# Moving the mixture stage's gathers, scatters and decode writes between queues and out of run-time branches

## The chip, the cores and the metric

The kernel runs on one core of a Trainium2 chip. The metric is device time in microseconds of one execution; the kernel before was executed three times, and its median is 681.64 us. One further execution was taken with the hardware profiler, and all rows below come from that one. A core has five instruction streams: PE (TensorE, matrix products and transposes), ACT (ScalarE), DVE (VectorE), POOL (GpSimd) and SP (SyncE, which here only starts transfers). Transfers are started from a queue of SP, of ACT or of POOL and run on 16 DMA engines that all queues share. Each stream works through its instructions in order and stands at the first one whose inputs are not there.

## What is computed

The reference is attention over a local window with a few global keys, then a mixture of eight experts, then a Fourier mixing step with a two-layer network. The change touches the mixture alone:

```python
logits = np.einsum('bsd,de->bse', x, w_gate)          # B=2, S=768, D=512, E=8
...
        p = softmax(logits[b, s])                      # e is the arg max, or the previous token's expert
        h = np.maximum(x[b, s] @ w1[e], 0.0)           # D -> F=1024
        out[b, s] = p[e] * (h @ w2[e])                 # F -> D
```

Which tokens go to which expert is known only at run time. For the network at the end, `w_ch1` and `w_ch2` arrive as 64-bit words that have to be decoded to 32-bit numbers.

## The kernel before, in words

Attention writes each token's row (512 numbers and the 8 probabilities) to a scratch tensor `xs` in device memory, and for every expert a list of its tokens. The mixture then runs expert by expert, `Moe.expert(e, n, more)` for e = 0 to 7 (called here e0 to e7), where `n` is the number of 128-token chunks that expert e has, as a register. In the profiled execution e1, e2, e3 and e5 have more than one chunk, e4 and e6 have one.

**Tokens.** `gathers(e)` (L1157) issues three indirect DMAs on POOL's queue (L1134), one per possible chunk, which bring the rows of expert e from `xs` into the tiles `xg`. Chunks 0 and 1 of every expert use the same two tiles; chunk 2 alternates between two. `tokens(e)` (L1171) transposes chunks 0 and 1 of `xg` on PE (L1165, four transposes each), splits the result into a high part on ACT (`xh`, L1168) and a low part on DVE (`xl`, L1169), copies the probabilities to `pc` on DVE (L1181) and, at its end, issues `gathers(e + 1)`. `tokens(e + 1)` runs as background work inside expert e, so `gathers(e + 2)` is issued inside expert e.

**Three branched parts.** For e1 to e6 an expert consists of three parts that are run-time branches (`tc.If`), each with an arm that is left out:

1. L1360 to L1363: with n > 1 `wide()`, the first product for 256 tokens (`first256`, L1224); else `narrow(y)`, which does both products for 128 tokens, and the next expert's `tokens` with them.
2. `third()` (L1292): the product `weight(e, (2,))`, a copy of `pc` by DVE, and with n > 2 a third chunk.
3. L1366 to L1369: with n > 1 `seconds(y, z)`, the second product of chunk 0 into the PSUM tile `y` and of chunk 1 into `z` (`second`, L1204), with `tokens(e + 1)` in the background; else one idle product into `z` (`keep_busy`, L50).

Behind the third part ACT scales `y` and `z` by `pc` into SBUF (`write`, L1187), and POOL scatters both to the result `x2` by indirect DMA (L1192).

**Weights.** `Ring` streams the weights through four staging buffers `raws` of 1 MB (`load`, on SP's queue, L987 for expert weights and L991 for the 64-bit words) in a fixed order. `take` splits an expert's 1 MB piece into two casts on ACT (L1049) and two subtractions on DVE (L1051), and then loads the piece four places on into the freed buffer. Expert e splits the weights of expert e + 1: those of the first product in part 1 (`first`), those of the second in part 3 (`then`). Eight pieces of 64-bit words are decoded in between (`d` units: ACT L1082, then DVE L1091, L1093, L1095 and L1097). A decoded piece, the tile `dec` of 512 KB with two buffers, is written to a scratch tensor `wmf` by a DMA on POOL's queue (L1015), behind the load that takes the freed staging buffer. Expert parts 1 of e1, e2, e3 and e5 end with such a piece, and parts 3 of e2 and e3 do.

The order in which instructions of background work stand between the products is the program's own: after every third product of the second stage, and twice per pair of 128-column blocks in the first, the background advances by fixed steps. In part 3 the order on ACT is: first cast of the piece, `xh` of chunk 0, second cast, `xh` of chunk 1, the other two casts, and the decode's first step.

Of the kernel before, what the change touches and what calls it, by code (L numbers as in the profile page):

```python
# [11 lines left out]
F32 = mybir.dt.float32  # L12
# [5 lines left out]
AF = mybir.ActivationFunctionType  # L18
# [27 lines left out]
def keep_busy(nc, st, ps, n):  # L46

    x = st.busy
    for _ in range(n):
        nc.tensor.matmul(ps, x[:, :1].to_broadcast([P, P]), x.unsqueeze(1).to_broadcast([P, 8, D]), start=True, stop=True)  # L50
# [887 lines left out]
class Ring:  # L938
# [63 lines left out]
    def take(self, kind, n, cols=1024, follow=True, eng=None, first=None, part=(0, 1), free=lambda: True):  # L1002

        nc = self.tc.nc
        r = self.at[kind, n]
        raw = self.st.raw[r % PIECES]
        if kind == "d":
            words, t = self.start(r)
            yield
            for k, _ in enumerate(self.bits(words, t)):  # L1010
                if k != 0:
                    yield
            self.load(r + PIECES)

            nc.gpsimd.dma_start(self.st.wm[n // 2, :, n % 2 * (PW // 2):(n % 2 + 1) * (PW // 2)], t)  # L1015
            return
        hi, lo = self.get(kind, n)
        w = TW if kind == "t" else PW
        if kind == "m" and MIX[n][0] >= EARLY:
            w = PW // 2  # L1020
            held = []

            def place():
                for k, t in held:
                    cs = slice(k * w, k * w + w)
                    nc.scalar.copy(hi[:, cs], t)
                    self.behind.append((lo[:, cs], t, hi[:, cs].bitcast(F32), n if k else None))
                held.clear()

            for k in range(2):  # L1030
                words, t = self.start(r + k)
                held.append((k, t))
                for j, cost in enumerate(self.bits(words, t)):
                    if j == 0:
                        self.small()
                    yield cost
                self.load(r + k + PIECES)
                yield 0
                if len(held) < 2:
                    self.start(r + k + 1)  # L1040
                if free():
                    place()
            while not free():
                yield 0
            place()
            return
        for c in range(int(part[0] * w), int(part[1] * w), cols):
            cs = slice(c, min(c + cols, w))
            (first or nc.scalar.copy)(hi[:, cs], raw[:, cs])  # L1049
            yield  # L1050
            (eng() if callable(eng) else eng or nc.vector).tensor_tensor(lo[:, cs], raw[:, cs], hi[:, cs].bitcast(F32), op=ALU.subtract)  # L1051
            yield
        if follow:
            self.load(r + PIECES)
# [46 lines left out]
class Moe:  # L1101
# [69 lines left out]
    def tokens(self, e):  # L1171
        for c in range(2):
            yield from self.turn(e % 2, c, self.place(e, c + (e == 0)))
            yield
        self.weight(e, range(2) if e else (1, 2))
        if e + 1 < E:
            self.gathers(e + 1)

    def weight(self, e, cs):
        for c in cs:  # L1180
# [81 lines left out]
    def expert(self, e, n, more):  # L1262
        tc, ring = self.tc, self.st.ring
        nc = tc.nc
        pc, ent = self.pc[e % 2], self.ent[e % 4]
        w1, w2 = rows(self.st, 4 * e), rows(self.st, 4 * e + 2)
        bg = Background()

        def chain(*gs):
            for g in gs:  # L1270
                yield from g


        at = 0 if e else 1
        step = lambda: bg.step(2)
        spare = self.ps_more, "more"

        def result(c, h, y, ys, *more):
            if isinstance(y, tuple):
                y = y[0].tile([P, DM], F32, name=y[1])  # L1280
            self.second(*h, w2, y, *more)
            bg.drain()
            if not ys:
                return
            last = e == LAST and c == 1
            write = lambda: self.write(y, pc[:, c:c + 1], ent[:, c, 1:2], ys, "first" if last else None)
            if last:
                self.finish = write
            else:
                write()  # L1290

        def third():  # L1292
            self.weight(e, (2,))

            with tc.If(n > 2):  # L1295
                if e < LAST:
                    for _ in self.turn(2, 0, self.place(e, 2)):
                        pass
                late = self.first128(w1, *self.more, spare, spare)
                result(2, self.more[1], spare, "more", lambda: None, late)  # L1300
                if e == LAST:
                    self.rest(more)

        own = lambda s, c: [t[:, :, c * P:(c + 1) * P] for t in s]
        hs = self.hh[0], self.hl[0]
        first, then = ([ring.take(*u, follow=e < LAST) for u in units] for units in ring.plan[e])

        def wide():
            bg.add(chain(*first))
            calls = iter(range(8))  # L1310
            n = 2 + (len(first) > 3)
            self.first256(e, lambda: bg.step(n) if e or next(calls) > 1 else None)
            bg.drain()

        def anew(units):
            for u in units:
                if u[0] == "d":
                    ring.begun.pop(ring.at[u], None)

        def narrow(y):  # L1320
            units = [u for part in ring.plan[e] for u in part]
            anew(units)
            takes = {u: ring.take(*u) for u in units}
            d = [takes[u] for u in units if u[0] == "d"]
            bg.add(chain(*(takes["e", 4 * e + 4 + k] for k in range(2))))
            h = own(hs, 0)
            late = self.first128(w1, own((self.xh[e % 2], self.xl[e % 2]), 0), h, (self.ps_h, "h"), (self.ps_x, "xtp"), bg.step,
                                 [self.place(e, 2)[:, :DM], self.work.tile([P, DM], F32, name="ys", bufs=2)])
            bg.drain()
            then = chain(*(takes["e", 4 * e + 6 + k] for k in range(2)), *d)  # L1330
            bg.add(then)
            calls = iter(range(8))

            def behind():
                if next(calls) == TOKENS:
                    bg.add(self.tokens(e + 1))
                bg.step()

            result(0, h, y, None, behind, late)

        def seconds(y, z):
            anew(ring.plan[e][1])
            bg.add(self.tokens(e + 1))
            bg.add(chain(*then))
            result(at, own(hs, 0), y, "" if e else "ys", step)
            if e:
                result(1, own(hs, 1), z, None)

        if e == 0:
            self.entries(2)  # L1350
            wide()
            seconds((self.ps_y, "y"), None)
            with tc.If(n > at + 1):
                result(at + 1, own(hs, 1), spare, "more")
            return
        if e < LAST:
            if e + 2 < E:
                self.entries(e + 2)
            y = self.ps_y.tile([P, DM], F32, name="y")
            with tc.If(n > 1) as arm:  # L1360
                wide()
            with arm.Else():
                narrow(y)  # L1363
            third()
            z = self.ps_more.tile([P, DM], F32, name="more")
            with tc.If(n > 1) as arm:  # L1366
                seconds(y, z)
            with arm.Else():
                keep_busy(nc, self.st, z, 1)  # L1369
            for c, t, k in ((0, y, "ys"), (1, z, "more")):  # L1370
                self.write(t, pc[:, c:c + 1], ent[:, c, 1:2], k)
            return

        bg.add(self.turn(2, 0, self.place(e, 2)))
        for c in range(2):
            x, h = (own(s, c) for s in ((self.xh[e % 2], self.xl[e % 2]), (self.hh[0], self.hl[0])))
            late = self.first128(w1, x, h, (self.ps_h, "h"), (self.ps_x, "xtp"), step, [x[:, :DM] for x in self.xg[:2]])
            if c == 0:
                third()
                bg.add(chain(*first))  # L1380
            result(c, h, (self.ps_y, "y"), "ys", step, late)
            if c == 0:
                self.fetch(0)
# [56 lines left out]
    def run(self):  # L1440
# [15 lines left out]
        keep_busy(nc, st, spare, WARM[1])  # L1456
        for _ in self.tokens(0):
            pass
        keep_busy(nc, st, spare, WARM[2])
        ring.load(2 * PIECES - 1, nc.scalar)  # L1460
        for e in range(E):
# [499 lines left out]
```

## Time and profile before

| | us |
|---|---|
| median of three runs | 681.64 |
| lowest and highest of them | 680.83, 793.94 |
| the profiled execution, whole time | 682.85 |
| its span, first to last instruction | 681.1 |
| PE busy in the span | 621.2 (91%) |
| DVE busy | 384.6 (56%) |
| ACT busy | 277.2 (41%) |
| POOL busy | 102.8 (15%) |

The span is what the rows below divide up; 1.75 us lie around it. A line of the timeline gives start, duration, engine, line, operation, output and input, and in brackets how long the engine had been idle and what released it. A line of the waits gives who waited for whom, the total, the number of times and the longest. A line of the windows gives a stretch, its length, the busy time and number of instructions of each engine, the granted TensorE clock (1.00 is 2.4 GHz, 0.50 is 1.2 GHz), the DMA engines' share and GB/s.

### The profile page before, as it was taken

To read this page: it belongs to the slowest core of one execution; us is meant where nothing else is said; L and a number is where in the kernel's file an instruction comes from. 1 tells how busy PE (TensorE), PEld (TensorE's weight loads), DVE (VectorE), ACT (ScalarE), POOL (GpSimd) and SP (SyncE) were. 2 spreads that over 40 slices of the span, in tenths; PEclk is the share of its full clock that TensorE was granted. 3 is DMA by queue.
4 is the path that set the end of the run, shared out by engine and by line. 5 is a ranking of instruction groups with operands and counts; after the bars stand their busy time and mean duration, and the time that the engine had idled before them with its cause. 6 is when DMAs were issued, how large, how long until landed. Compare 5 with 4: busy or idle time off the path is not lost. (4 is left out here: it accounts for less than half of the span.)

```text
span 681.1 us, 10013 instructions
## 1 busy us (share of the span) xinstructions
PE 621.2 (91%) x3508; PEld 502.4 (74%) x3509; DVE 384.6 (56%) x900; ACT 277.2 (41%) x550; POOL 102.8 (15%) x149
## 2 busy tenths in 40 slices
PE   8999998896777779649999999999999999999997
PEld 4777765686676767638777778788888888888886
DVE  5777766297365656444435998899752131254112
ACT  6799871263343437435443363344111131132110
POOL 2156623322202121203101000000000000000000
PEclk9999998998797979769899999999999999999999
DMA  7578832579465859446504415255010010100001
GB/s 272 186 177 225 163 111 46 188 277 385 162 196 191 271 187 332 145 156 234 188 5 187 154 55 176 85 192 204 31 63 1 0 63 1 62 1 0 1 0 63
DMA packets 25357, 92.56 MB, mean 136 GB/s; under 512 B 7805, under 2 KB 8957, under 8 KB 17345
## 3 DMA queue, kind: packets, MB, share of 16 engines
q1 hardware_dynamic: 19664, 79.50, 35.6%
q0 software_dynamic: 4896, 10.56, 4.3%
q10 hardware_dynamic: 720, 1.55, 0.6%
q8 instruction: 39, 0.64, 0.4%
q14 instruction: 38, 0.30, 0.2%
HBM read 81.00 MB, written 15.37 MB: 141 GB/s over the span
## 5 line engine op out<-in xcount | busy, mean ns | idle before, releaser
L1768 DVE SCALAR_TENSOR_TENSOR hl<-h,hh 128x512 fp32r<-128x512 f32 x48 | 33.1, 689 | 117.4 <-ACT hh L1767 117.4
L1767 ACT ACTIVATE hh<-h 128x512 fp32r<-128x512 f32 x48 | 28.8, 599 | 164.3 <-PE h L1763 164.3
L1051 DVE TENSOR_TENSOR wide<-raws,wide 128x1024 fp32r<-128x1024 f32 (+1 forms) x38 | 44.8, 1200 | 26.5 <-ACT wide L1049 26.5
L1049 ACT CAST wide<-raws 128x1024 fp32r<-128x1024 f32 (+2 forms) x42 | 40.7, 991 | 28.8 <-DMA raws<-we 24.7
L168 ACT ACTIVATE t<-t,nm 128x256 f32<-128x256 f32 (+1 forms) x96 | 45.8, 478 | 11.2 <-DVE nm L159 10.5
L1763 PE MATMUL h<-un0h,wide 128*128 128x512 f32 (+1 forms) x136 | 42.4, 378 | 0.1
L1134 POOL DMA_INDIRECT xg<-xs,ent x23 | 29.5, 1283 | 83.2 <-DVE pc L1181 71.9
L1165 PE MATMUL xtp<-consts,xg 128*128 128x128 f32 x64 | 13.2, 347 | 31.5 <-DMA wmf<-dec 29.3
L159 DVE CUSTOM_DVE_ANT_0 t<-sp,bias 128x256 f32<-128x256 f32 (+1 forms) x96 | 32.8, 398 | 8.8 <-PE sp L150 4.5
L1778 PE MATMUL acc<-wide,hh 128*128 128x512 f32 x96 | 37.8, 393 | 0.0
L1777 PE MATMUL acc<-wide,hh 128*128 128x512 f32 x96 | 37.6, 392 | 0.0
L1779 PE MATMUL acc<-wide,hl 128*128 128x512 f32 x96 | 37.5, 390 | 0.0
L1165 PEld LDWEIGHTS xtp<-consts,xg 128*128 128x128 f32 x64 | 10.2, 180 | 35.9 <-issue 34.7
L1169 DVE TENSOR_TENSOR xl<-xtp,xh 128x512 fp32r<-128x512 f32 x16 | 10.9, 688 | 40.6 <-ACT xh L1168 40.6
L1763 PEld LDWEIGHTS h<-un0h,wide 128*128 128x128 f32 x136 | 25.0, 188 | 5.0 <-ACT un0h L1538 0.3
L178 PE MATMUL tp<-consts,t 128*128 128x128 f32 x176 | 26.1, 283 | 1.7 <-ACT p L184 1.2
L1204 PE MATMUL y<-wide,hh 128*128 128x512 f32 x64 | 22.6, 476 | 5.1 <-PEq L1295 5.1
L178 PEld LDWEIGHTS tp<-consts,t 128*128 128x128 f32 x176 | 18.9, 140 | 9.3 <-ACT p L184 4.2
L1763 PE MATMUL h<-un0l,wide 128*128 128x512 f32 (+1 forms) x68 | 25.6, 377 | 0.0
L1224 PE MATMUL h<-xh,wide 128*128 128x256 f32 x160 | 24.0, 290 | 0.7 <-DVE pc L1181 0.7
L192 PE MATMUL sm<-p,vs 128*64 128x128 f32 x352 | 24.5, 279 | 0.0
L184 ACT COPY p<-tp 128x512 f32<-128x512 f32 (+1 forms) x48 | 24.2, 535 | 0.3 <-PE tp L178 0.3
(474 smaller groups left out, 1651.1 us busy)
## 6 DMA issues: line engine op xcount, KB each, us to landing
raws<-we SPq DMA_DIRECT2D x31, 1024.0 KB
raws<-wm SPq DMA_DIRECT2D x18, 1024.0 KB
raws<-wmf SPq DMA_DIRECT2D x7, 1024.0 KB
wmf<-dec POOLq DMA_DIRECT2D x8, 512.0 KB
xs<-xrow SPq DMA_DIRECT2D x12, 260.0 KB
vs<-v SPq DMA_DIRECT2D x6, 512.0 KB
raws<-kq SPq DMA_DIRECT2D x3, 1024.0 KB
u<-x SPq DMA_DIRECT2D x6, 512.0 KB
```

Source lines behind the costliest of these rows:

```text
L159: V.tensor_tensor_reduce(out=u.t[:, x, :u.W], in0=u.sp[:, j, k, :u.W], in1=bias[:, 4 * u.g + x, u.b0:u.b0 + u.W], scale=-0.125, scalar=3.0 ...
L168: A.activation(u.t[:, x, :u.W], u.t[:, x, :u.W], AF.Exp, bias=u.nm[:, x:x + 1], scale=-1.0, accum_out=u.den[:, x])
L178: T.transpose(u.tp[k][:, j, c], u.t[:, 2 * k + j, c * P:(c + 1) * P], st.ident)
L1049: (first or nc.scalar.copy)(hi[:, cs], raw[:, cs])
L1051: (eng() if callable(eng) else eng or nc.vector).tensor_tensor(lo[:, cs], raw[:, cs], hi[:, cs].bitcast(F32), op=ALU.subtract)
L1134: return self.tc.nc.gpsimd.indirect_dma_start(out=out, out_offset=None, in_=table, in_offset=bass.IndirectOffsetOnAxis(ap=idx, axis=0), bo ...
L1763: nc.tensor.matmul(ps[:, c], a[:, k], x[:, k, c], start=n == 0, stop=n == 11)
L1767: nc.scalar.activation(hh, ps, AF.Relu)
L1768: nc.vector.scalar_tensor_tensor(hl, ps, 0.0, hh.bitcast(F32), op0=ALU.max, op1=ALU.subtract)
L1777: T.matmul(acc[c], hh[:, cs], h2, start=first, stop=False)
L1778: T.matmul(acc[c], hh[:, cs], l2, start=False, stop=False)
L1779: T.matmul(acc[c], hl[:, cs], h2, start=False, stop=last)
```

## The change

The decode write goes through SP's queue. `tokens` no longer issues gathers; `gathers(1)` is issued behind `tokens(0)`, `gathers(2)` in e0 behind its second products, and `gathers(e + 2)` for e1 to e5 behind all three branched parts and ahead of the scatters. `z` is allocated and scaled into an SBUF tile `other` inside the arm that computes it; the other arm sets `other` to zero on DVE and has no product. The scatter of `other` follows that of `y`.

```diff
@@ Ring.take
             self.load(r + PIECES)
 
-            nc.gpsimd.dma_start(self.st.wm[n // 2, :, n % 2 * (PW // 2):(n % 2 + 1) * (PW // 2)], t)
+            nc.sync.dma_start(self.st.wm[n // 2, :, n % 2 * (PW // 2):(n % 2 + 1) * (PW // 2)], t)
             return
@@ Moe.tokens
         self.weight(e, range(2) if e else (1, 2))
-        if e + 1 < E:
-            self.gathers(e + 1)
@@ Moe.expert, e == 0
             seconds((self.ps_y, "y"), None)
+            self.gathers(2)
             with tc.If(n > at + 1):
@@ Moe.expert, 0 < e < LAST
             third()
-            z = self.ps_more.tile([P, DM], F32, name="more")
+            other = self.work.tile([P, DM], F32, name="more", bufs=1)
             with tc.If(n > 1) as arm:
+                z = self.ps_more.tile([P, DM], F32, name="more")
                 seconds(y, z)
+                nc.scalar.activation(other, z, AF.Copy, scale=pc[:, 1:2])
             with arm.Else():
-                keep_busy(nc, self.st, z, 1)
-            for c, t, k in ((0, y, "ys"), (1, z, "more")):
-                self.write(t, pc[:, c:c + 1], ent[:, c, 1:2], k)
+                nc.vector.memset(other, 0.0)
+            if e + 2 < E:
+                self.gathers(e + 2)
+            self.write(y, pc[:, 0:1], ent[:, 0, 1:2], "ys")
+            self.scatter(other, ent[:, 1, 1:2])
             return
@@ Moe.run
         for _ in self.tokens(0):
             pass
+        self.gathers(1)
         keep_busy(nc, st, spare, WARM[2])
```

## Rows read from the trace of the kernel before

**Rows 1.** Windows by expert (e0, e1, e2, e4, e5): PE, PEld, DVE, ACT, POOL, clock, DMA, GB/s

```profile
128.67:151.83 23.16, 23.16 (x153) 21.10 (x153) 19.06 (x27) 13.69 (x17) 6.63 (x5) 1.00 0.76 271
151.83:187.69 35.86, 26.04 (x153) 23.03 (x152) 19.43 (x23) 13.65 (x17) 10.46 (x11) 0.81 0.75 281
187.69:222.02 34.33, 25.93 (x153) 22.93 (x152) 20.81 (x25) 14.70 (x18) 6.58 (x6) 0.85 0.57 192
...
256.15:271.23 15.08, 13.43 (x66) 10.53 (x65) 11.87 (x14) 12.30 (x16) 2.55 (x2) 1.00 0.98 328
271.23:314.26 43.03, 28.41 (x153) 24.85 (x154) 17.22 (x22) 13.71 (x18) 10.14 (x10) 0.76 0.53 182
```

**Rows 2.** Waits within e1 to e6 (151.83 to 329.4 us)

```profile
DVE xl L1169 <- ACT xh L1168: 34.4, 8, 9.6
...
PE xtp L1165 <- DMA wmf<-dec: 29.3, 4, 9.3
ACT wide L1049 <- DMA raws<-we: 24.7, 3, 10.2
ACT more L1187 <- PE more L1204: 19.0, 4, 4.8
...
DVE wide L1051 <- ACT wide L1049: 15.0, 5, 7.4
...
DVE sl0l L1051 <- ACT sl0h L1049: 8.1, 3, 7.6
...
ACT xh L1168 <- PE xtp L1165: 6.2, 7, 2.1
PE h L1224 <- DVEq L1366: 6.1, 1, 6.1
...
PE more L50 <- ACTq L1366: 1.7, 2, 0.9
```

**Rows 3.** Timeline of PE in e2, part 3

```profile
208.41 1.08 PE L1165 MATMUL xtp<-consts,xg 128*128 128x128 f32 x4 [7.90 <-DMA wmf<-dec]
```

**Rows 4.** Timeline of POOL: last gather for e3, write in e2, last gather for e6

```profile
183.52 1.00 POOL L1134 DMA_INDIRECT xg<-xs,ent  x1 [0.30 <-ACT ys L1187]
...
200.98 0.60 POOL L1015 DMA_DIRECT2D wmf<-dec  x1 [11.07 <-DVE dec L1097]
...
274.58 1.01 POOL L1134 DMA_INDIRECT xg<-xs,ent  x1 [0.30 <-issue]
```

**Rows 5.** Timeline of SP's queue in e1 and e2

```profile
182.12 0.33 SPq L987 DMA_DIRECT2D raws<-we  x1
...
200.75 0.33 SPq L987 DMA_DIRECT2D raws<-we  x1
```

**Rows 6.** Timeline of ACT in e2, part 3

```profile
207.09 1.04 ACT L1049 CAST wide<-raws 128x1024 fp32r<-128x1024 f32 x1 [7.40 <-DMA raws<-we]
209.57 0.59 ACT L1168 CAST xh<-xtp 128x512 fp32r<-128x512 f32 x1 [1.44 <-PE xtp L1165]
```

**Rows 7.** Timeline of DVE in e2: part 1 from start to end, then part 3

```profile
189.66 1.23 DVE L1051 TENSOR_TENSOR sl0l<-raws,sl0h 128x1024 fp32r<-128x1024 f32 x1 [7.57 <-ACT sl0h L1049]
...
199.46 1.23 DVE L1097 SCALAR_TENSOR_TENSOR dec<-raws,dec 128x1024 int32<-128x1024 int32 x1
...
210.19 0.69 DVE L1169 TENSOR_TENSOR xl<-xtp,xh 128x512 fp32r<-128x512 f32 x1 [7.80 <-ACT xh L1168]
```

**Rows 8.** Timeline of DVE from e4's end into e5

```profile
270.94 0.20 DVE L1181 COPY pc<-xg 128x1 f32<-128x1 f32 x2
278.05 0.15 DVE L1181 COPY pc<-xg 128x1 f32<-128x1 f32 x1 [6.91 <-DMA xg<-xs,ent]
279.46 1.23 DVE L1051 TENSOR_TENSOR sl0l<-raws,sl0h 128x1024 fp32r<-128x1024 f32 x1 [1.25 <-DVEq L1366]
...
291.24 1.23 DVE L1097 SCALAR_TENSOR_TENSOR dec<-raws,dec 128x1024 int32<-128x1024 int32 x1
```

**Rows 9.** Windows of one us around the load's landing, columns as in rows 1

```profile
206.00:207.00 1.00, 0.00 (x0) 0.00 (x0) 0.00 (x0) 0.00 (x0) 0.00 (x0) 0.50 0.91 373
```

## Prediction

> **What bounds the kernel now.** I read the page's busy shares first, then windows by expert, then the waits within e1 to e6, then the timelines of all engines around one such wait. PE is busy 91% of the span, so the place to look is where it is not. In e0 PE works through all 23.16 us at clock 1.00; e1 does the same work in 35.86 us, e2 in 34.33 and e5 in 43.03, at clocks of 0.76 to 0.85 [rows 1] (e3 is like e2). With e4 and e6 at 15.08 each the stage takes 35.86 + 2 x 34.33 + 43.03 + 2 x 15.08 = 177.7 us.
>
> The largest wait of PE there is 29.3 us in four pieces: the transposes of the next expert's tokens, in part 3 of e1, e2, e3 and e5, wait for the decode write [rows 2]. They do not need it. In e2 they read rows whose last gather POOL had finished issuing at 184.5 us; the write was issued at 200.98 [rows 4], and PE started at 208.41, 7.90 us late [rows 3]. The reason is in the code: the narrow arm, not taken here but ahead of part 3 in the program, gathers into the same `xg` tiles from the same queue on which the taken arm writes its decoded piece. The wait has to hold for either arm and covers the write.
>
> A second wait ends almost as late, and the forecast hangs on it. ACT's first cast in part 3 of e2 starts at 207.09, after 7.40 us [rows 6], although the piece it splits was ordered at 182.12; what lands at 207 is the load ordered at 200.75 [rows 5], the last of part 1. Here too the narrow arm loads into the buffer that is read. Three such casts waited 24.7 us together [rows 2] and a fourth, in e3, about as long. DVE stands behind: its last decode step of part 1 ends at 200.69, its next large one starts at 210.19 [rows 7].
>
> So each wide expert has two chains. PE alone would need some 23.7 us (23.16 and a branch). ACT and DVE need part 1 (189.66 to 200.69, 11.0 us [rows 7]), the landing of a load, and part 3. Removing PE's wait moves the bound to the second chain, and I count what that one gains.
>
> **The change part by part.**
>
> *Decode writes on SP.* Eight issues leave POOL (0.60 us each [rows 4]) and come to SP, where an issue takes 0.33 [rows 5]. The write waits for the same decode step as the load just ahead of it, so it adds no wait of SP. Behind it stand the next loads, due only when the next piece has been split, 0.33 us later at worst. Bounds: nothing, and 8 x 0.33 = 2.6 us if each delay reached the path; I take nothing. If SP had to stand until something lands, that would be the slow rival below.
>
> *The transposes' wait.* With no gather in the narrow arm and no write on POOL's queue, the transposes wait only for gathers issued a whole expert earlier. PE's 29.3 us go, and with them the stretch at clock 0.50 that the idle leaves behind [rows 9]; but PE then runs ahead of ACT and DVE, so the second chain is what counts:
>
> - `xh` right behind the first cast: in e2 it waited 1.44 us for PE [rows 6], all such waits are 6.2 in seven [rows 2]. The small ones of these lie in e4 and e6, which change little: 5 us gained.
> - The start of the next part 1: ACT first has to scale `z`, and waited for PE's second product four times, 19.0 us [rows 2]; DVE's first subtraction waits for ACT's cast behind it, 15.0 + 8.1 = 23.1 us in eight, up to 7.57 [rows 2, 7]. With PE ahead, ACT still needs the scaling, the branch and one cast of 1.04 [rows 6]; I leave 1.5 us for each of the four long waits and 1 for the short ones: 23.1 - 7 = 16 us gained.
>
> The first cast's own wait stays: the order of the loads in either arm is unchanged.
>
> *Gathers behind the parts.* Three per expert, 1.00 us each [rows 4], move behind part 3 and ahead of two scatters. They are needed in the next expert's part 3, some 11 us later, or late in its narrow arm. The scatters go out later by as much; nobody waits for them before the mixer. Nothing at these two places. In e4 there is a gain: `third()` copies from an `xg` tile into which the narrow arm has just gathered e6's rows, so DVE waited 6.91 us for a landing, the last gather being issued at 274.58 [rows 4, 8], and PE 6.1 behind it [rows 2]. From 271.14 to 279.46 DVE did nothing else: 8.3 us [rows 8]. I leave 1.3 for the branch and ACT's cast: 7 us. And e5's part 1, begun with PE at clock 0.50 like all such stretches, took DVE 279.46 to 292.47, 13.0 us [rows 8], against 11.0 in e2: 2 us.
>
> *`other` and the idle product.* In the wide arm ACT does the same two scalings, that of `y` now second. In the narrow arm a product of PE and a scaling of ACT go, and DVE gains one zero fill of 128x512, which no row shows: between nothing, where DVE waits anyway, and 1.23, the duration of a 128x1024 subtraction [rows 7]; I take 0.5, twice. PE waited 1.7 us for the two idle products [rows 2]; e4's is inside the 7 us, e6's gives 1, less the fill: about 0.5 us.
>
> *Transfers, closer together.* The six experts move 10.1 + 2 x 6.6 + 7.8 + 2 x 4.95 = 41 MB [rows 1]. In some 150 us instead of 178 that is 275 GB/s, near e1's 281, where the first cast waited up to 10.2 us [rows 2] and not 7.4 [rows 6]. I charge this 2.8 us once (bounds: nothing, and all three other parts, 8.4).
>
> Sum: 5 + 16 + 7 + 2 + 0.5 - 0.5 (e4's fill) - 2.8 = 27.2, say 28 with the few short waits of `xh` behind the second cast. The profiled execution took 682.85 (span 681.1), the median is 1.2 below: 682.85 - 28 = 654.9, as a median 653.6 us. What follows the mixture is untouched and moves up as a block.
>
> One rule weighed against a row. The load ordered at 200.75 and the write at 200.98 moved together, the engines busy at 0.91 and 373 GB/s until 207 [rows 9]. The Trainium skill, DMA: Bandwidth & Descriptors, "Queues, rings and completion order", says that an engine takes turns between queues with work, and within one queue goes in ring order. By that rule the load, now ahead of the write in one ring, would land up to 0.5 MB / 373 GB/s = 1.4 us sooner (an estimate); four times that would make the sum 33 and the time 648. No row here shows the two on one queue, so I leave it out of the sum; it lies within the range.
>
> **The rivals.**
>
> *A. The second wait goes too* (0.14). If the casts no longer wait for the load, PE is the bound: e1, e2, e3 and e5 at 23.7 us instead of 147.6 together save 53. For it: e0, where PE never waits [rows 1]. Against: the loads keep their order, and 41 MB at e4's 328 GB/s, a share of 0.98 [rows 1], take 125 us by themselves, so not all can be had. I price it at 42 us: 640.
>
> *B. Transfers take half* (0.18). e1 already moves 281 GB/s [rows 1]; if its part gains nothing (its share of the 16 is 6 us, from 7.57 to 1.5) and the other three wait as it does (8.4 for the 2.8), 28 - 6 - 5.6 = 16 remain: 666.
>
> *C. It does not do what it says* (0.06). The third part keeps a scatter in its branch, so the transposes could go on waiting for POOL's queue. Then only the e4 terms stand, 7 + 2: 674, within 2%. Against it: the wait names the write, and the write has left that queue.
>
> *D. SP becomes the bound: slower* (0.04). If SP must stand at each write until the load ahead of it has landed, 6.3 us (200.75 to 207 [rows 5, 9]), no later load is ordered meanwhile. Eight times 6.3 is 50 us, against 28 gained: 704. It decides from 28 / 8 = 3.5 us per write. Against it: the same instruction releases load and write, and SP's next load in e2 came only after the casts. For it: with the experts closer together the slack ahead of that load is gone.
>
> **How the numbers follow.** The forecast has 0.58. Its own range is 644 to 663: the bounds above, 8.4 for 2.8 on one side, the rule's 5 us and the short waits on the other. To hold 8 of 10, the range reaches most of the way to A and past B: 634 to 669. A measurement of this kernel can tell about 2%, 13.6 us, from no change. Faster by more than that (below 668): the forecast, A and most of B, 0.58 + 0.14 + 0.14 = 0.86. Within 2%: the rest of B and C, 0.10. Slower: 0.04, D.
>
> **What would show it.** Right: no transposes waiting for a DMA in part 3 of e1, e2, e3 and e5; clock near 1.00 there; ACT's first cast still released by `raws<-we`, 6 to 9 us after the last load's order; DVE the engine that PE now waits for early in part 1; no wait of DVE's `pc` copy between e4 and e5; everything from e7 on some 28 us earlier. Wrong: that first cast starting with part 3 (A), a later landing in every expert (B), transposes still released by a DMA (C), gaps between SP's issues behind the writes with idle DMA engines (D).

## The result, and the profile after

The changed kernel takes 648.72 us (median of four runs, 645.75 to 649.89) against 681.24 for the kernel before, run on the same chip: a ratio of 0.953 with a 95% interval of 0.948 to 0.957. One execution of the kernel before took 793.94 us; the ratio leaves it out. Forecast were 653.6, with 644 to 663 as the likeliest case's own range. The profiled execution took 645.75 us, 3 below its median; 682.85 - 645.75 makes 37.1, of which 2.2 lie ahead of e0 (it starts at 126.52, before at 128.67), 33.9 between the starts of e0 and e7, and 1.0 behind.

The page after, its span, PE's share and the granted clock in 40 slices:

```profile
span 644.0 us, 9941 instructions
...
PE 612.6 (95%) x3506; PEld 495.6 (77%) x3507; DVE 383.9 (60%) x902; ACT 273.5 (42%) x548; POOL 101.8 (16%) x141
...
PEclk9999998999999888999999999999999999999999
```

The windows by expert, e1 to e6, columns as in [rows 1]:

```profile
149.69:175.34 25.65, 23.44 (x153) 21.13 (x152) 15.58 (x18) 11.75 (x16) 3.79 (x4) 1.00 0.77 300
175.34:200.40 25.06, 23.46 (x153) 20.90 (x151) 15.82 (x21) 12.33 (x18) 6.94 (x5) 1.00 0.73 261
200.40:230.49 30.09, 25.36 (x153) 22.90 (x154) 20.35 (x26) 14.14 (x19) 6.43 (x5) 0.94 0.74 266
230.49:252.27 21.78, 15.11 (x65) 11.36 (x64) 20.18 (x26) 15.92 (x22) 7.35 (x5) 0.91 0.85 301
252.27:277.87 25.60, 24.93 (x153) 22.53 (x154) 13.92 (x18) 10.84 (x15) 5.91 (x5) 0.94 0.71 247
277.87:293.27 15.40, 13.28 (x65) 10.31 (x64) 15.29 (x20) 13.28 (x18) 6.71 (x5) 1.00 0.87 315
```

Against [rows 1], e1 is 10.2 us shorter, e2 9.3 and e5 17.4; e3 is 4.0 shorter (34.13 before), e6 0.3 longer, and e4 6.7 longer. e1 and e2 run at clock 1.00, before at 0.81 and 0.85.

The waits within e1 to e6, the ones that answer to [rows 2]:

```profile
DVE xl L1169 <- ACT xh L1168: 35.4, 4, 9.7
...
ACT wide L1049 <- DMA raws<-we: 19.5, 3, 9.7
...
ACT wide L1049 <- PE more L1202: 10.0, 1, 10.0
ACT sl0h L1049 <- PE more L1202: 9.0, 1, 9.0
...
ACT more L1185 <- PE more L1202: 4.8, 1, 4.8
...
PE h L1222 <- DVE pc L1179: 4.3, 1, 4.3
PE h L1222 <- DVE wide L1051: 4.2, 1, 4.2
...
DVE wide L1051 <- ACT wide L1049: 0.2, 1, 0.2
```

The transposes' 29.3 us are gone, and so are DVE's 23.1 us for a cast (0.2 left of 15.0 in the last line) and `xh`'s 6.2. DVE's 34.4 for the first `xh` of a part 3 is 35.4 now. What holds it is ACT's first cast of part 3, which waited 9.74, 10.03, 8.95 and 8.06 us in e1, e2, e3 and e5: lines 2 to 4, of whose 19.5 us 1.7 lie in e4. Two of the four are put down to PE's `more`; the experiments show that this is not what they wait for. PE waits for DVE's subtraction, 4.2 us, in e3 alone and in the middle of part 1; foreseen was a wait early in it.

The timeline of part 3 of e2, all engines:

```profile
188.80 0.60 PE L1165 MATMUL xtp<-consts,xg 128*128 128x128 f32 x4
...
189.19 0.33 SPq L987 DMA_DIRECT2D raws<-we  x1
189.57 0.43 SPq L1015 DMA_DIRECT2D wmf<-dec  x1
...
197.38 1.05 ACT L1049 CAST wide<-raws 128x1024 fp32r<-128x1024 f32 x1 [10.03 <-PE more L1202]
...
198.95 0.69 DVE L1169 TENSOR_TENSOR xl<-xtp,xh 128x512 fp32r<-128x512 f32 x1 [9.17 <-ACT xh L1168]
```

PE transposes right at the start of part 3, without the 7.90 us of [rows 3]. The cast starts 8.2 us after the last load of part 1 was ordered, and DVE stands 9.17 us for it. PE works on: its products of part 3 need neither.

### The profile page after: what moved, and what is told of

It is laid out like the page before. It is cut to its first block, busy times and chain, and to the rows that moved or that the text cites. A ratio compares the mean times of both kernels' runs of the same rounds, so it can differ in the third digit from the quotient of the medians.

```text
span 644.0 us, 9941 instructions
## 1 busy us (share of the span) xinstructions
PE 612.6 (95%) x3506; PEld 495.6 (77%) x3507; DVE 383.9 (60%) x902; ACT 273.5 (42%) x548; POOL 101.8 (16%) x141
## 4 chain that ended last, share of the span: by engine, by line
PE 49%; DVE 1%; issue 0%; ACT 0%; DVEq 0%; ACTq 0%
PE h L1767 21%; PE acc L1782 7%; PE acc L1781 7%; PE acc L1783 7%; PE y L1202 1%; PE acc L1601 1%; PE acc L1587 1%; PE h L1252 1%; PE f L1733 1%; PE f L1630 1%; PE h L50 1%; PE f L1652 0%; DVE u L1792 0%; PE acc L1590 0%; PE f L1633 0%; PE acc L1652 0%
## 5 line engine op out<-in xcount | busy, mean ns | idle before, releaser
L1049 ACT CAST wide<-raws 128x1024 fp32r<-128x1024 f32 (+2 forms) x42 | 40.7, 993 | 34.1 <-DMA raws<-we 19.5
L1134 POOL DMA_INDIRECT xg<-xs,ent x23 | 31.4, 1367 | 105.9 <-DVE pc L1179 63.6
L1222 PEld LDWEIGHTS h<-xh,wide 128*128 128x128 f32 x160 | 21.4, 196 | 4.9 <-ACT ys L1185 4.7
L1097 DVE SCALAR_TENSOR_TENSOR dec<-raws,dec 128x1024 int32<-128x1024 int32 x18 | 22.1, 1226 | 0.6
L1095 DVE SCALAR_TENSOR_TENSOR dec<-raws,dec 128x1024 int32<-128x1024 int32 x18 | 22.0, 1223 | 0.4
```

The lines of the kernel that those rows point to most:

```text
L1134: return self.tc.nc.gpsimd.indirect_dma_start(out=out, out_offset=None, in_=table, in_offset=bass.IndirectOffsetOnAxis(ap=idx, axis=0), bo ...
L1222: T.matmul(ps[:, u], w[:, f], x[:, k], start=n == 0, stop=n == 11)
```

## The experiments

Each was timed beside the kernel before on one chip, and its ratio is against those runs. The name in brackets is the one used further on. First the change's three edits one by one.

**Only the queue of the writes** (queue_alone).

```diff
-            nc.gpsimd.dma_start(self.st.wm[n // 2, ...], t)
+            nc.sync.dma_start(self.st.wm[n // 2, ...], t)
```

> The kernel before with only the decode writes moved to SP's queue; gathers, scatters and the idle product stay. My theory: the 29.3 us that PE's transposes waited in e1, e2, e3 and e5 covered the write alone, so they go, and with them what the changed kernel gained there; the wait of DVE's pc copy between e4 and e5 (8.3 us without work on DVE, 7 of it gained by the whole change, and 2 of e5's pace) stays, since that one is for gathers. 681 - 32.5 + 9 = 657 us (654 to 661), no transposes waiting for a DMA in part 3 of the four wide experts. Rival one, the gathers in the arm not taken hold the transposes just as well without the write, so both edits are needed: 675 or more. Rival two, the gathers' place carries everything: 681, no change.

657.68 us, ratio 0.966 [0.962, 0.971]. Waits of PE and DVE in e1 to e6:

```profile
DVE xl L1169 <- ACT xh L1168: 37.6, 4, 9.7
DVE pc L1181 <- DMA xg<-xs,ent: 8.7, 1, 8.7
...
PE h L1224 <- DVEq L1366: 7.5, 1, 7.5
```

No transposes wait in part 3; the wait for gathers between e4 and e5 stays, 8.7 us with PE's 7.5 behind it. As expected, within a microsecond.

**Only the gathers' place** (gathers_alone).

```diff
@@ tokens
-        if e + 1 < E:
-            self.gathers(e + 1)
@@ expert, behind the three parts
+            if e + 2 < E:
+                self.gathers(e + 2)
             for c, t, k in ((0, y, "ys"), (1, z, "more")):
```

(and `gathers(1)`, `gathers(2)` as in the change)

> The kernel before with only the gathers moved behind the three branched parts; decode writes stay on POOL's queue, the idle product stays. My theory: the wait exists because the arm not taken gathers into the rows that the transposes read; with no gather in that arm nothing ties the transposes to POOL's queue, so PE's 29.3 us go here too, and the wait between e4 and e5 goes as well: 650 us (647 to 654), as good as the whole change. Rival one, the write must leave POOL's queue for that: only the 9 us between e4 and e5, 672. Rival two, the gathers now stand behind a 512 KB write in one queue and come late for the next transposes: 660 or more, with transposes that wait for gathers.

656.04 us, 0.964 [0.959, 0.968]: outside my 647 to 654, on the way to the second rival's 660. The transposes of part 3 in e1, e2, e3 and e5 no longer wait for the write, though it is still on POOL's queue (one, in e1, waits 1.90 us for gathers). But POOL and PE show, at the end of e3 and in e4:

```profile
243.18 0.57 POOL L1015 DMA_DIRECT2D wmf<-dec  x1 [19.39 <-DVE dec L1097]
244.27 1.85 POOL L1134 DMA_INDIRECT xg<-xs,ent  x1 [0.52 <-DMA raws<-we]
...
253.05 1.09 PE L1165 MATMUL xtp<-consts,xg 128*128 128x128 f32 x4 [5.27 <-DMA xg<-xs,ent]
```

The write of e3's part 3 stands ahead of the gathers on POOL and waits 19.39 us for DVE's last decode step, so the gathers go out at 244.27, 9.5 us behind e4's start (234.79), and e4's transposes wait 5.27 us for them. In the changed kernel, where POOL has no write to stand for, the same gathers go out 3.1 us behind it (233.60 and 230.49). Either edit alone takes away the transposes' wait for the write; by the ratios, each is some 5 to 7 us short of both together (two_edits, below).

**Only the last edit** (zero_alone). `z` scaled inside its arm, a zero fill in the other, no idle product, the scatters in the new order.

> The kernel before with only the last edit: z scaled inside the arm that computes it, a zero fill in the other arm, no idle product, the scatters in the new order. My theory: about nothing, 680.7 us (679 to 682): e6 loses a product (1 us) and gains a fill (0.48 us in the changed kernel), and e4's stands inside a wait that stays. Rival: the idle product and the scaling behind it are what held e5's start, so the 8.3 us between e4 and e5 shrink: 674.

681.90 us, 1.003 [1.000, 1.006]: nothing, as expected. Its waits in e1 to e6 keep the four long ones:

```profile
PE xtp L1165 <- DMA wmf<-dec: 29.7, 4, 9.4
```

**Both first edits without the last** (two_edits).

> The kernel before with the decode writes on SP's queue and the gathers behind the three parts, but with the idle product and the scaling of z as before. Alone, the last edit measured 1.0029 [1.0, 1.0058]. My theory: it is worth half a us at most in either direction here too, so the first two edits together are the whole gain: 649 us (646.5 to 651). Rival: once PE's waits are gone, the idle product and its scaling in e4 and e6 stand on ACT's chain, which is then the bound, and leaving them out is worth 2 us in each: 653 or more.

650.03 us, 0.956 [0.952, 0.960], beside 0.953 [0.948, 0.957] for the whole change: not to be told apart. The two edits are the gain.

**The second wait** (late_loads). In the narrow arm, the loads behind the two pieces that the wide arm splits in part 3 are moved to the other arm of part 3. The wide arm's own code is not touched.

```diff
@@ narrow
+            held = [("e", 4 * e + 6 + k) for k in range(2)]
-            takes = {u: ring.take(*u) for u in units}
+            takes = {u: ring.take(*u, follow=u not in held) for u in units}
@@ the other arm of part 3
                 nc.vector.memset(other, 0.0)
+                for k in range(2):
+                    ring.load(ring.at["e", 4 * e + 6 + k] + PIECES)
```

> The changed kernel with the narrow arm's loads behind the two pieces that the wide arm splits in part 3 moved out of the narrow arm, into the other arm of part 3, so that no load of the arm not taken touches the buffer that ACT's first cast of part 3 reads. My theory: that cast waits for the last load of part 1 only because of that arm; it then starts with part 3, DVE's wait of 35.4 us in four for the cast ahead of xh goes, and PE becomes the bound of e1, e2, e3 and e5: 23.7 us each instead of 29.3 + 29.6 + 30.4 + 25.3 = 114.6, so up to 19 us; less 4 for loads of e4 and e6 that go out later: 635 us (630 to 642). Rival one, the transfers set the pace (DMA share 0.72 to 0.74 in these experts) and the wait comes back in front of the next part's casts: 645 to 649. Rival two, the later loads of e4 and e6, where the share is 0.93 to 1.00, cost more than that: slower than the changed kernel, 650 or more.

638.10 us, 0.939 [0.935, 0.943]. Its windows of e1, e2, e3, e4 and e5, DVE's wait in these, and the first cast in e2:

```profile
150.66:176.31 25.65, 23.44 (x154) 21.14 (x153) 19.36 (x23) 12.85 (x16) 7.16 (x7) 1.00 0.98 367
176.31:200.10 23.79, 23.28 (x154) 21.06 (x152) 17.86 (x23) 14.34 (x18) 5.89 (x5) 1.00 0.79 259
200.10:223.90 23.80, 23.29 (x153) 21.07 (x152) 19.50 (x24) 14.46 (x18) 6.41 (x5) 1.00 0.94 333
223.90:241.25 17.35, 13.04 (x65) 10.42 (x64) 15.59 (x19) 13.30 (x18) 3.54 (x2) 0.94 0.94 334
241.25:268.85 27.60, 25.76 (x153) 23.39 (x154) 17.31 (x22) 11.60 (x15) 8.86 (x8) 0.91 0.78 266
```

```profile
DVE xl L1169 <- ACT xh L1168: 3.5, 4, 1.5
```

```profile
188.74 1.05 ACT L1049 CAST wide<-raws 128x1024 fp32r<-128x1024 f32 x1 [0.44 <-ACTq L1293]
```

The cast starts with part 3, ahead of the last load's order (189.63 here). 35.4 us of DVE's wait became 3.5, and e2 and e3 take 23.8 us, PE alone; e1 and e5 keep 2 and 4 us above that, which is why it is 638 and not 635. So the cast waited neither for its own data nor for PE's product, as the rows after had it in two cases. It waited for the last load of part 1, and only because the arm not taken loads into the buffer that the cast reads.

**The same edit in the kernel before** (late_before).

> The kernel before with only the narrow arm's two loads moved into the other arm of part 3 (the edit of late_loads); gathers, writes and idle product as before. My theory of two chains: the transposes go on waiting for the decode write, in e2 to 208.4 us, 1.3 us behind the cast that is set free, so PE's wait of 29 us stays; the cast and its subtraction are done ahead of xh, which spares about 1.5 us in each of four experts: 675 us (671 to 679), against 11 us that the same edit gave behind the change. Rival: the cast's wait was the real bound in the kernel before, the transposes' wait stood beside it: 665 or less.

679.94 us, 1.000 [0.998, 1.003]: no gain at all, outside my 671 to 679. In e2 the cast is free and `xh`, behind it, is not; the waits of PE in e1 to e6 come behind the two rows:

```profile
198.72 1.05 ACT L1049 CAST wide<-raws 128x1024 fp32r<-128x1024 f32 x1 [0.44 <-ACTq L1295]
208.09 0.59 ACT L1168 CAST xh<-xtp 128x512 fp32r<-128x512 f32 x1 [8.33 <-PE xtp L1165]
```

```profile
PE xtp L1165 <- DMA wmf<-dec: 31.9, 4, 9.7
```

The two waits stood side by side. Taking away the second alone moves nothing, since PE still waits 31.9 us for the write and then has all of its own work to do; behind the change the same edit is worth some 10 us. The 1.5 us per expert that I had counted for ACT and DVE did not reach the time.

**Write and load exchanged** (write_first). In the changed kernel, the decode write is issued ahead of the load.

```diff
-            self.load(r + PIECES)
             nc.sync.dma_start(self.st.wm[n // 2, ...], t)
+            self.load(r + PIECES)
```

> The changed kernel with the decode write issued ahead of the load on SP's queue, not behind it. The Trainium skill (DMA: Bandwidth & Descriptors, Queues, rings and completion order) has one queue go in ring order. If the cast in part 3 waits for that load and the ring goes in order, the load lands behind 0.5 MB more, 1.4 us later in each of four experts (0.5 MB at 373 GB/s): 654 us (652 to 656). If what moves at one time shares the engines whatever the order, nothing: 649 (647 to 650). A third way: what the cast waits for goes by the place of a transfer in the arm (the third of either arm), so that it now waits for the write, 512 KB, which lands first: 2 us sooner in each of four experts, 641 (638 to 645), with wmf<-dec named as what released the cast.

646.91 us, 0.949 [0.945, 0.954]: by the time not to be told from the changed kernel, and outside the third way's 638 to 645. The waits in e1 to e6 tell more:

```profile
DVE xl L1168 <- ACT xh L1167: 22.8, 4, 6.9
...
ACT wide L1048 <- DMA wmf<-dec: 16.2, 3, 5.9
...
ACT sl0h L1048 <- DMA wmf<-dec: 7.7, 1, 7.7
```

All four first casts are now released by the write, which they have no use for; it is the third transfer of the wide arm here, as the load was, and the third of the narrow arm is the load into the cast's buffer. That was the third way. Its price was wrong: the casts do start earlier, 4.8 us in the mean after the write's order (163.16 to 168.04, 188.97 to 193.65, 215.15 to 221.16, 263.05 to 266.56), and e5 starts at 247.67 and not at 252.27, but then e5 and e6 take 45.5 us instead of 41.0. e5 begins after 6.06 us without work on PE (4.33 in the changed kernel), at a clock of 0.50. At the start of its part 3 PE stops once more. The timeline of PE at these two places, each with the window behind it:

```profile
247.67 2.04 PE L1221 MATMUL h<-xh,wide 128*128 128x256 f32 x8 [6.06 <-DVE pc L1178]
...
265.53 0.38 PE L1164 MATMUL xtp<-consts,xg 128*128 128x128 f32 x2 [2.49 <-issue]
```

```profile
247.60:250.00 2.40, 2.33 (x11) 2.36 (x12) 1.37 (x3) 0.72 (x1) 0.04 (x1) 0.50 0.93 321
...
266.00:268.00 2.00, 2.00 (x9) 1.67 (x8) 0.00 (x0) 1.44 (x3) 0.00 (x0) 0.56 0.82 303
```

For the stop in part 3 the profile has no releaser, and a clock of 0.56 follows it. It is not of this one execution alone: late_loads, executed twice under the profiler, stops at the same place in e5, for 1.32 and 1.75 us, also without a releaser. What PE waits for there stays open.

**The narrow arm's tokens sooner** (late_early). In the kernel with late loads the narrow arm begins the next expert's tokens at the first background step of its second product instead of the fifth (`TOKENS` 0 for 4).

> The kernel late_loads with the next expert's tokens started at the first step of the second product in the narrow arm and not at the fifth (TOKENS 0 for 4), so that xh and xl of chunk 0 come ahead of the cast that waited 3.1 us for a load in e4. My theory: PE's last wait of this kind, 4.3 us at the start of e5 for the pc copy behind xl, shrinks to about 1: 634.5 us against 638 (633 to 637). Rival: e5 then waits for the split weights instead, that is for the same load, or xh ahead of the casts delays these: 638 or more.

634.88 us, 0.934 [0.930, 0.938]. e5's start, which had waited 4.31 us for `pc` in late_loads:

```profile
241.74 0.48 PE L1222 MATMUL h<-xh,wide 128*128 128x256 f32 x2 [1.45 <-PEq L1366]
```

Both were run once more, beside each other on one chip (late_loads_again, late_early_again), with a third kernel that has the sooner tokens but not the late loads (after_early).

> The changed kernel with only the tokens of the narrow arm started four steps sooner (TOKENS 0 for 4), the narrow arm's loads where they were. My theory: as in late_early, PE starts e5 some 3 us sooner (in the changed kernel it waited 4.33 us for the pc copy), and e7 1 us: 645.5 us against 648.7 (643 to 648). Rival: what e5 gains at its start it gives back at its part 3, where the cast waits for a load that is not due sooner: 648 to 650.

648.28 us, 0.958 [0.953, 0.963]: nothing, as the rival had it. From e0's to e5's start it took 123.8 us against 125.8 after, and from there to e7's 43.1 against 41.0.

> The kernel of late_loads once more, beside late_early on one chip, since the two were timed on different ones: 638.1 us there, ratio 0.9388 [0.9348, 0.9427]. If that holds, 0.939 again.

637.35 us, 0.939 [0.936, 0.942]. Its own rows differ from the first time in two places. e1 takes 27.5 us, and not the 25.65 shown above; and at e5's start PE waits

```profile
241.02 1.76 PE L1222 MATMUL h<-xh,wide 128*128 128x256 f32 x8 [2.07 <-DVE pc L1179]
```

and not 4.31. So most of what late_early seemed to gain at that place lies between two executions of one kernel.

> The kernel of late_early once more, beside late_loads on one chip. The profiles say that the earlier tokens gain 2.1 us from e4's to e5's start and 1.3 from there to e7's, but e1 and e2 took 1.9 us longer though no instruction of theirs was changed. If that was chance of one execution, late_early is 3 us ahead: a ratio 0.934 to 0.935. If it belongs to the kernel, 1 to 1.5 us ahead: 0.937.

635.91 us, 0.937 [0.933, 0.941]. The longer e1 and e2 do not belong to the sooner tokens, since late_loads_again has them too. In both pairs of traces e5 and e6 together take 1.2 to 1.3 us less with the sooner tokens (41.4 against 42.7). The late loads are sure; a microsecond or so on top, from the sooner tokens, is not separated by these intervals. This kernel has the lowest time found, and its interval lies below the changed kernel's.

## Why the prediction came out

The forecast's mechanism was right and its time 5 us too long. One term was sized 6.5 us too small, and two smaller misses went the other way.

**What bounds.** That a second chain stands behind PE's wait and becomes the bound held: DVE's wait for `xh` stayed (34.4 and 35.4), and late_loads and late_before, one edit worth some 10 us behind the change and nothing ahead of it, show both halves of it.

**The transposes.** All of the 29.3 us went, by either of the first two edits. The reason given, that the arm not taken ties the transposes to what the taken arm has on the same queue, is what queue_alone and gathers_alone show together.

**`xh` behind the first cast**, 5 us: 6.2 went.

**The start of the next part 1**, 16 of 23.1: this is the term that was mis-sized. Nearly all went, 22.5; a new wait of 1.5 us, in e4, is behind a load. I had left 1.5 us at each of the long waits for ACT to scale `z` and to cast. From e1 to e2 the rows after are

```profile
176.24 0.69 ACT L1368 ACTIVATE more<-more,pc 128x512 f32<-128x512 f32 x1
...
177.39 1.06 ACT L1049 CAST sl0h<-raws 128x1024 fp32r<-128x1024 f32 x1
```

```profile
176.65 2.35 DVE L1051 TENSOR_TENSOR sl5l<-raws,sl5h 128x1024 fp32r<-128x1024 f32 x2
178.91 1.22 DVE L1051 TENSOR_TENSOR sl0l<-raws,sl0h 128x1024 fp32r<-128x1024 f32 x1
```

ACT scales and casts while DVE still has two subtractions of part 3 to do. Where the late chain is the bound, its backlog covers what used to be its wait.

**e4 to e5**, 7: DVE, without a large operation for 8.3 us before, now stands 1.0 us and fills for 0.48, as forecast:

```profile
251.98 0.27 DVE L1179 COPY pc<-xg 128x1 f32<-128x1 f32 x3
253.28 0.48 DVE L1370 MEMSET more<- 128x512 f32 x1 [1.03 <-ACT sl0h L1049]
```

In queue_alone, which lacks this term, DVE has no large operation there for 10.1 us (254.26 to 264.33). That run came out 9 us above the change, as I had expected from 7 + 2; since the 2 of the next term did not come, that it was 9 is in part luck.

**e5's pace**, 2: wrong. DVE's part 1 of e5 takes 253.68 to 267.76, 14.1 us against 13.0 before. I had taken the low clock there as gone with the idle time. But PE still stands at e5's start. The profile puts that down to the `pc` copy, which DVE makes behind the last `xl`, though the products that PE begins with read `xh` and weights alone. Then PE starts at half speed:

```profile
252.27 0.55 PE L1222 MATMUL h<-xh,wide 128*128 128x256 f32 x1 [4.33 <-DVE pc L1179]
```

```profile
252.27:256.30 4.03, 4.03 (x23) 4.03 (x24) 1.56 (x2) 0.66 (x1) 1.43 (x2) 0.65 0.94 370
```

The clock is 0.50 in the first two of these us, 0.59 in the third and 1.00 in the fourth.

**Transfers**, -2.8: from the end of DVE's last decode step to the cast it is 8.8, 8.3, 8.7 and 6.1 us in e1, e2, e3 and e5, before 9.2, 6.4, 6.0 and 6.2. That is 4.0 more in sum, in e2 and e3. In these two the engines moved 309 and 303 GB/s in that stretch, before 244 and 253; in e1 and e5, where it grew no longer, 265 and 256, before 271 and 249. That busier transfers are the cause is not shown: in e2 of gathers_alone the stretch took 9.7 us at 204 GB/s.

**The last edit**, +0.5 and -0.5: the fill took 0.48 us twice, and the edit came to nothing by two runs.

With these sizes the terms make 6.2 + 22.5 + 7 - 1.1 - 4.0, some 31 of the 33.9 us of the profiled execution; the other 3 are in no term, and that execution was 3 below the median of its kernel.

One thing was not foreseen: where the delay of the second chain falls. PE runs e1 and e2 at nearly its own pace, since its products there need what was split an expert earlier. It pays in e3 (4.2 us in the middle of part 1, for a subtraction) and in e4, 21.78 us and 15.08 before.

**The rivals.** A, the second wait gone, was not this change; late_loads made it so and came to 638, for which A had 640. B: e1's transfers cost nothing (8.8 us to the cast, before 9.2), though it was to be the one that gains nothing. C: `third()`'s scatter holds no transposes. D: SP's write issues took 0.42 to 1.12 us each, not the 3.5 from which that rival decides. C's 674 was worked out from the profiled time; from the median, as for the others, 9 us less make 672.6. Nothing hangs on it.

**The rule.** The Trainium skill, DMA: Bandwidth & Descriptors, "Queues, rings and completion order", has one queue go in ring order; by that I had estimated the load 1.4 us sooner when the write stands behind it in the same queue. The runs neither bear it out nor rule it out. two_edits and gathers_alone differ in the write's queue alone: from the last decode step to the cast it is 7.8 us in the mean of the four experts with the write behind the load in SP's queue, and 8.25 with it in POOL's, 0.4 us and a third of the estimate. queue_alone and the kernel before differ in the same thing, and there it is 8.5 and 6.9, the other way. write_first, where the write goes ahead and the cast is let go after 4.8 us, does not decide: a transfer half the size, ordered first, would land first under either theory.

## What to carry to other kernels

Where a kernel has run-time branches, look at every long wait behind a branch for what the arm *not* taken does to the same buffer or queue: a release by a transfer that the waiting instruction has no use for is the sign of it, and in late_loads, moving the other arm's transfers behind the branch took the wait away without touching the arm that runs. Before counting such a wait as gain, look at what ends next to it. Here two waits ended 1.3 us apart: taking away the cast's alone was worth nothing (late_before), the transposes' alone some 22 us (queue_alone), and the cast's was worth 10 us once the change had taken away the other. And when the bound moves to a chain of other engines, don't leave small waits in it that its own backlog will cover.

## What the runs showed besides

- A wait is named after what came last by the profile, not after what was needed: two of the four casts after were put down to PE's `more`, and all four went when a load was moved.
- A transfer that waits on POOL held up the ones queued behind it: with a write that stood 19.39 us for DVE ahead of them, gathers that needed nothing of it went out 6.4 us later behind the expert's start (9.5 against 3.1), and PE waited 5.27 us for them.
- After 4.33 us without work PE's next four us ran at a mean clock of 0.65, between its two levels of 0.50 (1.2 GHz) and 1.00 (2.4 GHz). Four us at 0.65 do the work of 2.6, so this wait cost 1.4 us more than its length.
